# An output product by Strassen's seven products and a mask moved to GpSimd, in a fused sparse-attention and bilinear-FFN kernel

## The chip, the cores and the metric

The kernel runs on one core of one Trainium2 chip. The metric is device time in microseconds. A run more than 1.5% above the fastest of the same kernel counts as slow. Differences from a kernel with slow runs are taken from the mean of its fast runs.

## The reference, cut to what matters

```python
# 8 batches, 8 heads, 576 positions, head size 64
mask_local   = (rel >= 0) & (rel < 32)                      # heads 0 to 3
mask_strided = (rel >= 0) & (pos_k % 32 == pos_q % 32)      # heads 4 to 7
x = softmax(mask(q @ k.T / 8)) @ v        # as 4608 tokens x 512
a, b = x @ w_a, x @ w_b                   # 512 -> 1536
return (a * b) @ w_out                    # 1536 -> 512
```

## The kernel before

The FFN runs in nine tiles of 512 tokens. A tile has sixteen steps: twelve "ab" steps (two products of 128 features, eight matmuls of 512 columns; ScalarE copies one, VectorE multiplies the copy with the other in PSUM and writes `pf` in bf16) and four output steps (twelve matmuls each, ScalarE evicts, a DMA stores). The attention of batch t+1 is woven into tile t: S steps (scores, exponential on ScalarE, mask on VectorE) and V steps (product with v, logarithm and exponential on ScalarE for the reciprocal of the sum, two multiplies on VectorE into `xT`). VectorE also transposes the queries and keys of one batch further on. In the timelines each engine runs its instructions in the order of the program: in tile 4 VectorE stood idle for 2.61 us until the multiplies of a V step started at 198.96, and the transpose behind them, whose input had been loaded by about 187.2 (issued at 183.83, 3.4 us to landing at most), followed at 199.91. In this kernel matmul results go to PSUM, in buffers called banks below; to evict is to copy a result from there to SBUF, where the kernel has its operands.

```python
def S_m(b, u):                                   # mask: and with 0 / -1
    ...
    nc.vector.tensor_tensor(pi, pi, mk, op=ALU.bitwise_and)

def step_VT(b, u):
    ...                                          # matmuls into o (one buffer)
    nc.scalar.activation(r, sums, ACT.Ln)
    nc.scalar.activation(r, r, ACT.Exp, scale=-1.0)
    for j in range(2):
        ...
        nc.vector.tensor_mul(dst..., o..., r[:, j])   # into xT

def ffn_ab(t, f, mid, ab=None):
    ...
    a_sb = fsb.tile([128, TTOK], F32, tag="a_sb", name="a_sb")
    nc.scalar.copy(a_sb, ab[0])
    nc.vector.tensor_mul(pf[:, f, :], a_sb, ab[1])

def ffn_y(t, j, mid):
    ...
        y = psum4["mm"].tile([128, n], F32, tag="mm", name="mm")
        for f in range(FD):
            nc.tensor.matmul(y, lhsT=pf[:, f, 128 * j:128 * (j + 1)], rhs=wo_sb[:, f, c0:c0 + n], ...)
    ...
```

The softmax here doesn't subtract the row's maximum and nothing guards it: scores larger than these inputs give would overflow.

Of the kernel before, what the change touches and what calls it, by code (L numbers as in the profile page):

```python
# [7 lines left out]
F32 = mybir.dt.float32  # L8
BF16 = mybir.dt.bfloat16
I16 = mybir.dt.int16  # L10
ALU = mybir.AluOpType
# [13 lines left out]
VW = 128  # L25
WCH = (0, 2, 5, 8, 10, 12)


@with_exitstack
def kernel(  # L30
# [55 lines left out]
    mask_l = const.tile([128, 4, LW], I16)  # L86
    mask_s = const.tile([NP, NP], I16)
    nmask = const.tile([NP, NP], BF16, name="nmask")

# [66 lines left out]
    cur = {}  # L156
    xT = const.tile([128, KD, n_tok], BF16)
    wa_sb = wp.tile([128, KD, d_ff], BF16)
    wb_sb = wp.tile([128, KD, d_ff], BF16)
    wo_sb = wp.tile([128, FD, d_model], BF16)  # L160

    tl = {}
# [4 lines left out]

    nats = {}

    def load_qk(b, strided, heads=range(HL), names="kq"):  # L170
        for nm in names:
            src = {"k": k, "q": q}[nm]
            if b < FIRST_D:
                n, R, h0 = (NP, RS, HL) if strided else (96, RL, 0)
                if (b, nm, strided) not in nats:
                    nats[b, nm, strided] = nat.tile([n, HL, R, D], BF16, tag=f"{nm}{R}", name=f"{nm}{R}", bufs=1)
                t = nats[b, nm, strided]
                hs = slice(heads[0], heads[-1] + 1)
                nc.gpsimd.dma_start(out=t[:, hs], in_=src[b, h0:h0 + HL].rearrange("h (p r) d -> p h r d", r=R)[:, hs])
            elif strided:  # L180

                t = nat_s[nm]
                n = 32 if b == FIRST_D else YS
                for h in heads:
                    nc.gpsimd.dma_start(  # L185
                        out=t[32 * h:32 * h + n],
                        in_=bass.AP(tensor=src.tensor, offset=(b * H + HL + h) * S * D,
                                    ap=[[RS * D, n], [YS * RS * D, 3], [1, RS * D]]))
            else:
                if 0 in heads:  # L190
                    nats[b, nm, strided] = nat.tile([128, NY, D], BF16, tag=f"{nm}l", name=f"{nm}l")
                t = nats[b, nm, strided]
                for h in heads:
                    nc.gpsimd.dma_start(out=t[32 * h:32 * h + 32],  # L194
                                        in_=src[b, h].rearrange("(i y) d -> y i d", y=32))
            nats[b, nm, strided] = t
# [153 lines left out]
    def S_m(b, u):  # L350
# [4 lines left out]
        else:  # L355
            mk = mask_s.unsqueeze(1).unsqueeze(1).to_broadcast([NP, 2, G, n])
        pi = p[:M, :, :W].bitcast(I16).rearrange("p t (g n) -> p t g n", n=n)
        nc.vector.tensor_tensor(pi, pi, mk, op=ALU.bitwise_and)  # L358
# [68 lines left out]
    def step_VT(b, u):  # L427
# [21 lines left out]
        for j in range(2):  # L449
            dst = xT[64 * j:64 * j + 64, c, S * b:S * (b + 1)]  # L450
            if c < 2:
# [14 lines left out]
    def X_e(b, c):  # L466
        n = LW if c < 2 else NP
        tp = held.pop((b, "x", c))
        tv = tp.rearrange("d (g p) -> d g p", p=n)
        dst = xT[:, c, S * b:S * (b + 1)]  # L470
        if c >= 2:
# [39 lines left out]
    pfs = {}  # L511

    def ab_mm(t, f, ab, kks, mid=None, first=0, last=KD - 1):
        for w, ps_ in zip((wa_sb, wb_sb), ab):
            if mid and ps_ is ab[1]:
                mid()
            for kk in kks:
                nc.tensor.matmul(ps_, lhsT=w[:, kk, 128 * f:128 * (f + 1)], rhs=xT[:, kk, TTOK * t:TTOK * (t + 1)],  # L518
                                 start=(kk == first), stop=(kk == last))

    def ffn_ab(t, f, mid, ab=None):
# [3 lines left out]
        if ab is None:  # L525
            ab = [psum4["mm"].tile([128, TTOK], F32, tag="mm", name="mm") for _ in range(2)]
            if f == 0:
# [7 lines left out]
        nc.scalar.copy(a_sb, ab[0])  # L535
        nc.vector.tensor_mul(pf[:, f, :], a_sb, ab[1])  # L536
        return pf[:1, f, :1]

    def ffn_y(t, j, mid):
# [3 lines left out]
        for z, n in enumerate((256, 128, 128) if (t, j) == (NT - 1, 3) else (d_model,)):  # L543
            y = psum4["mm"].tile([128, n], F32, tag="mm", name="mm")
            for f in range(FD):
                nc.tensor.matmul(y, lhsT=pf[:, f, 128 * j:128 * (j + 1)], rhs=wo_sb[:, f, c0:c0 + n],  # L546
                                 start=(f == 0), stop=(f == FD - 1))
                if f == FD // 2 - 1:
                    mid()
            y_sb = fsb.tile([128, n], F32, tag="y_sb", name="y_sb", bufs=3)  # L550
            act = t < NT - 1 or (j + z) % 2 == 1
# [7 lines left out]
    with tc.manual_schedule(engines={ENG.PE, ENG.SP, ENG.Pool, ENG.DVE, ENG.Activation}):  # L559
# [71 lines left out]
        for t in range(NT):  # L631
            slots += [(ffn_ab, t, f) for f in range(FD)] + [(ffn_y, t, j) for j in range(4)]
        steps = {}
# [13 lines left out]
        for b in range(FIRST_D, B):  # L647
# [12 lines left out]
            for (z, nm, part), g in zip(((0, "k", 0), (0, "k", 1), (0, "q", 0), (0, "q", 1), (1, "k", 0), (1, "k", 1),  # L660
                                         (1, "k", 2), (1, "q", 0), (1, "q", 1), (1, "q", 2)), gs):
                do(g0 + g, step_D, b, z, nm, part)
        do(0, nc.vector.tensor_copy, mask_s, mss)
        for h in range(HL):
            do(6 + h, spread_vs, 1, h, nc.scalar.copy)
# [5 lines left out]
        for i, t in ((0, vl_buf[0]), (0, vs_buf[0]), (18, vl_buf[1]), (19, vs_buf[1])):  # L671
            do(i, fill_v, t)
        for i, (fn, t, j) in enumerate(slots):
            mid = lambda: take(i - 0.5)
            done = fn(t, j, mid) if fn is ffn_y else fn(t, j, mid, first.get(j) if t == 0 else None)
            if i > 13 and i in at:
# [33 lines left out]
```

## Time and profile before

| | before |
|---|---|
| time, median of 3 | 343.75 us (342.25 to 344.11) |
| TensorE busy | 333.1 us, 98% of the span |
| VectorE, ScalarE, GpSimd busy | 205.1, 203.9, 140.4 us |
| a tile with attention (tile 4): length, VectorE busy | 35.45, 24.80 us |
| a tile without (tile 7) | 31.08, 8.25 us |
| output phase of a tile without attention | 10.36 us |

TensorE is the bound; the other engines matter where TensorE waits for them. The lines are in the prediction.

### The profile page before, as it was taken

How to read it: one execution, taken by the hardware profiler on the slowest of the kernel's cores; microseconds unless marked ns; L12 is line 12 of the kernel's file. 1: busy time of each engine (PE TensorE's matmuls, PEld its weight loads, DVE VectorE, ACT ScalarE, POOL GpSimd, SP SyncE). 2: the span in 40 equal slices, each digit the busy share in tenths (PEclk: the TensorE clock that was granted, in tenths of full speed). 3: DMA queues.
4: the chain of work that ended last, by engine and by line, in shares of the span. 5: the costliest groups of instructions: out<-in, count | busy, mean ns of one | idle time of the engine just before them, and what ended most of it. 6: DMA issues, size and time to landing. Idle time of an engine off the chain costs nothing.

```text
span 341.5 us, 6887 instructions
## 1 busy us (share of the span) xinstructions
PE 333.1 (98%) x2520; PEld 173.7 (51%) x2520; DVE 205.1 (60%) x400; ACT 203.9 (60%) x331; POOL 140.4 (41%) x247
## 2 busy tenths in 40 slices
PE   8999999989989999999999999999999999999995
PEld 6754555445545555555555555555555444444444
DVE  6866657758759766876578846885666333303331
ACT  5754865368767765876587657775688533223311
POOL 8945539898537434653465346633000000000000
PEclk9999999999999999999999999999999999999999
DMA  9999999997999599969997989888220110021002
GB/s 160 154 203 197 202 176 172 179 154 89 129 200 101 90 99 185 99 110 91 165 104 133 77 168 96 132 80 145 76 59 2 61 63 0 0 92 34 0 31 94
DMA packets 102242, 37.56 MB, mean 110 GB/s; under 512 B 77632, under 2 KB 97728, under 8 KB 102208
## 3 DMA queue, kind: packets, MB, share of 16 engines
q0 software_dynamic: 87760, 19.58, 63.7%
q1 hardware_dynamic: 14304, 17.47, 16.2%
q8 instruction: 20, 0.33, 0.4%
q14 instruction: 14, 0.11, 0.1%
q10 hardware_dynamic: 144, 0.07, 0.1%
HBM read 39.71 MB, written 9.44 MB: 144 GB/s over the span
## 4 chain that ended last, share of the span: by engine, by line
PE 70%; DMA 17%; SPq 3%; DVE 3%; ACT 3%; POOL 2%; issue 2%; DVEq 0%; ACTq 0%
PE mm L518 41%; PE mm L546 20%; DMA vl<-in_v_dram 4%; PE o L438 3%; PE st L340 3%; DMA k<-in_k_dram 3%; DMA wa_sb<-in_moe_w_a_dram 3%; SPq L302 2%; DMA qz01l<-tq 2%; PE misc L153 2%; DMA out_dram<-y_sb 1%; DMA qz01s<-tq 1%; ACT xr L447 1%; DMA qz11s<-tq 1%; DVE tq L283 1%
## 5 line engine op out<-in xcount | busy, mean ns | idle before, releaser
L518 PE MATMUL mm<-xT,wb_sb 128*128 128x512 bf16 x424 | 110.1, 379 | 0.3
L518 PE MATMUL mm<-xT,wa_sb 128*128 128x512 bf16 x424 | 110.2, 379 | 0.1
L536 DVE TENSOR_TENSOR pf<-a_sb,mm 128x512 bf16<-128x512 f32 x106 | 71.9, 678 | 48.3 <-PE mm L518 25.5
L546 PE MATMUL mm<-wo_sb,pf 128*128 128x512 bf16 (+2 forms) x456 | 99.6, 368 | 0.1
L535 ACT COPY a_sb<-mm 128x512 f32<-128x512 f32 x106 | 62.1, 586 | 45.4 <-PE mm L518 43.0
L518 PEld LDWEIGHTS <-wb_sb 128*128 128x128 bf16 x432 | 41.7, 98 | 49.5 <-issue 1.3
L546 PEld LDWEIGHTS <-pf 128*128 128x128 bf16 x456 | 41.5, 98 | 42.3 <-issue 0.4
L518 PEld LDWEIGHTS <-wa_sb 128*128 128x128 bf16 x432 | 38.1, 98 | 34.2 <-issue 0.2
L552 ACT COPY y_sb<-mm 128x512 f32<-128x512 f32 (+2 forms) x35 | 20.0, 571 | 46.6 <-PE mm L546 38.6
L348 ACT ACTIVATE p<-st 128x576 bf16<-128x576 f32 (+1 forms) x64 | 41.7, 651 | 8.8 <-PE st L340 8.2
L447 ACT ACTIVATE xr<-o 64x576 f32<-64x576 f32 x48 | 31.1, 647 | 23.5 <-PE o L438 23.3
L454 DVE TENSOR_TENSOR xT<-o,xr 64x288 bf16<-64x288 f32 x48 | 21.6, 450 | 33.1 <-ACT xr L448 32.8
L448 ACT ACTIVATE xr<-xr 64x576 f32<-64x576 f32 x48 | 32.8, 682 | 1.5
L452 DVE TENSOR_TENSOR xT<-o,xr 64x288 bf16<-64x288 f32 x48 | 21.6, 450 | 16.9 <-ACT xr L448 16.4
L678 POOL CAST pace<-pf 1x1 f32<-1x1 bf16 x51 | 11.6, 227 | 41.5 <-DVE pf L536 41.3
L358 DVE TENSOR_TENSOR p<-p,mask_l 128x576 int16<-128x576 int16 x32 | 14.6, 455 | 17.1 <-ACT p L348 17.1
L218 POOL DMA_DIRECT2D vs<-in_v_dram x24 | 19.6, 817 | 9.9 <-issue 9.9
L194 POOL DMA_DIRECT2D kl<-in_k_dram x24 | 16.0, 666 | 6.7 <-issue 5.0
L194 POOL DMA_DIRECT2D ql<-in_q_dram x24 | 16.0, 666 | 6.6 <-DMA wo_sb<-in_moe_w_out_dram 3.8
L185 POOL DMA_DIRECT2D natk<-in_k_dram x24 | 14.6, 610 | 3.6 <-issue 3.0
L185 POOL DMA_DIRECT2D natq<-in_q_dram x24 | 14.6, 609 | 0.0
L678 POOL COPY pace<-y_sb 1x1 f32<-1x1 f32 x22 | 4.2, 189 | 24.2 <-ACT y_sb L552 24.2
(116 smaller groups left out, 316.2 us busy)
## 6 DMA issues: line engine op xcount, KB each, us to landing
out_dram<-y_sb SPq DMA_DIRECT2D x35, 256.0 KB, 2.4
vl<-in_v_dram POOLq DMA_DIRECT2D x7, 384.0 KB, 6.6
kl<-in_k_dram POOLq DMA_DIRECT2D x24, 72.0 KB, 2.8
ql<-in_q_dram POOLq DMA_DIRECT2D x24, 72.0 KB, 3.3
vs<-in_v_dram POOLq DMA_DIRECT2D x24, 72.0 KB, 3.6
wo_sb<-in_moe_w_out_dram POOLq DMA_DIRECT2D x4, 384.0 KB, 11.9
natk<-in_k_dram POOLq DMA_DIRECT2D x20, 72.0 KB, 3.3
natq<-in_q_dram POOLq DMA_DIRECT2D x20, 72.0 KB, 3.3
```

The lines of the kernel that those rows point to most:

```text
L185: nc.gpsimd.dma_start(out=t[32 * h:32 * h + n], in_=bass.AP(tensor=src.tensor, offset=(b * H + HL + h) * S * D, ap=[[RS * D, n], [YS * RS ...
L194: nc.gpsimd.dma_start(out=t[32 * h:32 * h + 32], in_=src[b, h].rearrange("(i y) d -> y i d", y=32))
L348: nc.scalar.activation(p[:M, :, :W], st[:M, :, :W], ACT.Exp, scale=scale)
L447: nc.scalar.activation(r, sums, ACT.Ln)
L448: nc.scalar.activation(r, r, ACT.Exp, scale=-1.0)
L452: nc.vector.tensor_mul(dst[:, W * half:W * (half + 1)], o[:64, j, :W], r[:, j])
L454: nc.vector.tensor_mul(dst.rearrange("d (p r) -> d p r", r=RS)[:, :, G * half:G * (half + 1)], o[:64, j, :W].rearrange("d (g p) -> d p g", ...
L518: nc.tensor.matmul(ps_, lhsT=w[:, kk, 128 * f:128 * (f + 1)], rhs=xT[:, kk, TTOK * t:TTOK * (t + 1)], start=(kk == first), stop=(kk == last))
L535: nc.scalar.copy(a_sb, ab[0])
L536: nc.vector.tensor_mul(pf[:, f, :], a_sb, ab[1])
L546: nc.tensor.matmul(y, lhsT=pf[:, f, 128 * j:128 * (j + 1)], rhs=wo_sb[:, f, c0:c0 + n], start=(f == 0), stop=(f == FD - 1))
L552: (nc.scalar.copy if act else nc.vector.tensor_copy)(y_sb, y)
```

## The change

The intent is to take an eighth of the multiplications out of the output product. Strassen's method splits a product into 2 x 2 blocks and forms it from seven block products of sums of blocks. Here the rows (tokens) are split in two, the 1536 features in even and odd groups of 128, the output columns in two halves. Sums of the weights are made once; sums of `pf` and the combination of the seven results are new work for VectorE and GpSimd. To relieve VectorE, the mask of the strided heads moves to GpSimd as a multiplication. To find room, `xT` becomes a ring of four batches; the matmul results get a fourth PSUM bank. (The prediction's count of time T starts at 0 with a tile's output phase, its last four steps; so does T below.)

```diff
         nc.scalar.copy(a_sb, ab[0])
-        nc.vector.tensor_mul(pf[:, f, :], a_sb, ab[1])
+        if t in FAST_Y:                                      # (1, ..., 8)
+            halves = lambda x: x.rearrange("p (m i) -> p m i", i=2)
+            nc.vector.tensor_mul(pf[:, f, :].rearrange("p (i m) -> p m i", i=2), halves(a_sb), halves(ab[1]))
+        else:
+            nc.vector.tensor_mul(pf[:, f, :], a_sb, ab[1])
...
+        if b >= FIRST_D and c >= 2:                          # in the mask step
+            pm = p[:M, :, :W].rearrange("p t (g n) -> p t g n", n=n)
+            nc.gpsimd.tensor_tensor(pm, pm, mask_b..., op=ALU.mult)
+            return
...
+        if n == 0:                                           # sums of pf, a third of the features at a time
+            nc.gpsimd.tensor_tensor(s[:, :, 0:HT], x[:, :, 0, 0], x[:, :, 1, 1], op=ALU.add)
+        elif n == 1:
+            nc.vector.tensor_tensor(s[:, :, HT:3 * HT]..., x[:, :, 0], x[:, :, 1], op=ALU.add)
+        else:
+            nc.vector.tensor_tensor(s[:, :, 3 * HT:]..., x[:, :, :, 1], x[:, :, :, 0], op=ALU.subtract)
...
+            rows = out[TTOK * t:TTOK * (t + 1), HN * j:HN * (j + 1)].rearrange("(q p i) c -> p i q c", q=2, i=2)
...
+            elif k == "4":                                   # w = P4 + P3, before P2 is added in bank b
+                v["w"] = v["a"]
+                nc.vector.tensor_tensor(v["w"], bank["b"], v["a"], op=ALU.add)
...
+        for k, b, lhs, rhs in (("3", "a", full(0, 0), wsum(0)), ("4", "b", full(1, 1), wsum(1)), ("1", "c", summed(0), wsum(2)),
+                               ("2", "b", summed(2), wfull(0, 0)), ("5", "a", summed(1), wfull(1, 1)),
+                               ("6", "c", summed(3), wsum(3)), ("7", "d", summed(4), wsum(4))):
```

The two halves of the rows are the even and the odd tokens of a tile. That is why the multiply goes through `pf` in the order m, i: two neighbouring inputs go to places 256 elements (512 bytes) apart.

More of the change, by code (lines that the diff above doesn't have):

```diff
@@ L26 @@
 WCH = (0, 2, 5, 8, 10, 12)
+FAST_Y = (1, 2, 3, 4, 5, 6, 7, 8)
 @with_exitstack
@@ L87 @@
     mask_s = const.tile([NP, NP], I16)
+    mask_b = const.tile([NP, NP], BF16)
     nmask = const.tile([NP, NP], BF16, name="nmask")
@@ L156 @@
     cur = {}
-    xT = const.tile([128, KD, n_tok], BF16)
+    XR = 4
+    xT = const.tile([128, KD, XR * S], BF16)
     wa_sb = wp.tile([128, KD, d_ff], BF16)
@@ L160, with fast_w @@
     wo_sb = wp.tile([128, FD, d_model], BF16)
+    FG = FD // 2
+    HT = TTOK // 2
+    HN = d_model // 2
+    wf = wp.tile([128, 5, FG, HN], BF16, name="wf")
+    wov = wo_sb.rearrange("p (g e) (j n) -> p e j g n", e=2, j=2)
+    def fast_w(n, gs):
+        a, b, op = ((wov[:, 0, 1], wov[:, 1, 1], ALU.subtract), (wov[:, 1, 0], wov[:, 0, 0], ALU.subtract),
+                    (wov[:, 0, 0], wov[:, 1, 1], ALU.add), (wov[:, 0, 0], wov[:, 0, 1], ALU.add),
+                    (wov[:, 1, 0], wov[:, 1, 1], ALU.add))[n]
+        nc.vector.tensor_tensor(wf[:, n, gs], a[:, gs], b[:, gs], op=op)
     tl = {}
@@ L168 @@
     nats = {}
+    shared = {}
     def load_qk(b, strided, heads=range(HL), names="kq"):
@@ L174, in load_qk @@
                 n, R, h0 = (NP, RS, HL) if strided else (96, RL, 0)
-                if (b, nm, strided) not in nats:
-                    nats[b, nm, strided] = nat.tile([n, HL, R, D], BF16, tag=f"{nm}{R}", name=f"{nm}{R}", bufs=1)
-                t = nats[b, nm, strided]
+                w0 = {"k6": 0, "q6": 1536, "k8": 3072, "q8": 5120}[f"{nm}{R}"]
+                if b not in shared:
+                    shared[b] = nat.tile([128, 5 * FD * TTOK // 4], BF16, tag="shared", name="shared")
+                t = nats[b, nm, strided] = shared[b][:n, w0:w0 + HL * R * D].rearrange("p (h r d) -> p h r d", r=R, d=D)
                 hs = slice(heads[0], heads[-1] + 1)
@@ L356, in S_m @@
             mk = mask_s.unsqueeze(1).unsqueeze(1).to_broadcast([NP, 2, G, n])
+        if b >= FIRST_D and c >= 2:
+            pm = p[:M, :, :W].rearrange("p t (g n) -> p t g n", n=n)
+            nc.gpsimd.tensor_tensor(pm, pm, mask_b.unsqueeze(1).unsqueeze(1).to_broadcast([NP, 2, G, n]), op=ALU.mult)
+            return
         pi = p[:M, :, :W].bitcast(I16).rearrange("p t (g n) -> p t g n", n=n)
@@ L449, in step_VT @@
         for j in range(2):
-            dst = xT[64 * j:64 * j + 64, c, S * b:S * (b + 1)]
+            dst = xT[64 * j:64 * j + 64, c, S * (b % XR):S * (b % XR + 1)]
             if c < 2:
@@ L469, in X_e @@
         tv = tp.rearrange("d (g p) -> d g p", p=n)
-        dst = xT[:, c, S * b:S * (b + 1)]
+        dst = xT[:, c, S * (b % XR):S * (b % XR + 1)]
         if c >= 2:
@@ L511, with mm_bank @@
     pfs = {}
+    used = [0]
+    def mm_bank(shape):
+        nm = "tp" if used[0] % 4 == 3 and used[0] >= 0 else "mm"
+        used[0] += 1
+        return psum4[nm].tile(shape, F32, tag=nm, name="mm")
     def ab_mm(t, f, ab, kks, mid=None, first=0, last=KD - 1):
+        n = min(TTOK, XR * S - TTOK * t % (XR * S))
+        cuts = [(0, n)] + ([(n, TTOK - n)] if n < TTOK else [])
         for w, ps_ in zip((wa_sb, wb_sb), ab):
@@ L517, in ab_mm @@
             for kk in kks:
-                nc.tensor.matmul(ps_, lhsT=w[:, kk, 128 * f:128 * (f + 1)], rhs=xT[:, kk, TTOK * t:TTOK * (t + 1)],
-                                 start=(kk == first), stop=(kk == last))
+                for c0, n in cuts:
+                    x0 = (TTOK * t + c0) % (XR * S)
+                    nc.tensor.matmul(ps_[:, c0:c0 + n], lhsT=w[:, kk, 128 * f:128 * (f + 1)], rhs=xT[:, kk, x0:x0 + n],
+                                     start=(kk == first and c0 == 0), stop=(kk == last and c0 == cuts[-1][0]))
     def ffn_ab(t, f, mid, ab=None):
@@ L525, in ffn_ab @@
         if ab is None:
-            ab = [psum4["mm"].tile([128, TTOK], F32, tag="mm", name="mm") for _ in range(2)]
+            ab = [mm_bank([128, TTOK]) for _ in range(2)]
             if f == 0:
@@ L535, in ffn_ab, with fast_s @@
         nc.scalar.copy(a_sb, ab[0])
-        nc.vector.tensor_mul(pf[:, f, :], a_sb, ab[1])
-        return pf[:1, f, :1]
+        if t in FAST_Y:
[3 more added lines that the diff above has]
+            nc.vector.tensor_mul(pf[:, f, :], a_sb, ab[1])
+        return pf[:1, f, :1]
+    pss = {}
+    def fast_s(t, n, gs):
+        if t not in pss:
+            pss[t] = nat.tile([128, 5 * FD * TTOK // 4], BF16, tag="shared", name="ps").rearrange("p (g m) -> p g m", g=FG)
+        s = pss[t][:, gs]
+        x = pfs[t].rearrange("p (g e) (i m) -> p g e i m", e=2, i=2)[:, gs]
+        if n == 0:
+            nc.gpsimd.tensor_tensor(s[:, :, 0:HT], x[:, :, 0, 0], x[:, :, 1, 1], op=ALU.add)
+        elif n == 1:
+            nc.vector.tensor_tensor(s[:, :, HT:3 * HT].rearrange("p g (i m) -> p g i m", i=2), x[:, :, 0], x[:, :, 1], op=ALU.add)
+        else:
+            nc.vector.tensor_tensor(s[:, :, 3 * HT:].rearrange("p g (e m) -> p g e m", e=2), x[:, :, :, 1], x[:, :, :, 0],
+                                    op=ALU.subtract)
@@ new lines, with y_plan, f32t, store @@
+    yst = {}
+    def y_plan(t):
+        pf, s = pfs[t], pss[t]
+        full = lambda e, i: (lambda g, q: pf[:, 2 * g + e, HT * i + 128 * q:HT * i + 128 * (q + 1)])
+        summed = lambda n: (lambda g, q: s[:, g, HT * n + 128 * q:HT * n + 128 * (q + 1)])
+        wsum = lambda n: (lambda g: wf[:, n, g])
+        wfull = lambda e, j: (lambda g: wov[:, e, j, g])
+        bank = {}
+        v = {}
+        def f32t(nm, bufs):
+            return fsb.tile([128, 2, HN], F32, tag=nm, name=nm, bufs=bufs)
+        def store(y, i, j, q=slice(0, 2), n=slice(0, HN)):
+            rows = out[TTOK * t:TTOK * (t + 1), HN * j:HN * (j + 1)].rearrange("(q p i) c -> p i q c", q=2, i=2)
+            nc.sync.dma_start(out=rows[:, i, q, n], in_=y[:, q, n])
+        def post(k):
+            if k == "3":
+                v["a"] = f32t("ya", 1)
+                nc.scalar.copy(v["a"], bank["a"])
+            elif k == "4":
+                v["w"] = v["a"]
+                nc.vector.tensor_tensor(v["w"], bank["b"], v["a"], op=ALU.add)
+            elif k == "1":
+                v["e"] = f32t("ye", 1)
+                nc.vector.tensor_tensor(v["e"], bank["c"], v["w"], op=ALU.add)
+            elif k == "2":
+                v["y21"] = f32t("y_sb", 4)
+                nc.scalar.copy(v["y21"], bank["b"])
+                store(v["y21"], 1, 0)
+                v["h"] = v["w"]
+                nc.gpsimd.tensor_tensor(v["h"], v["w"], v["y21"], op=ALU.subtract)
+            elif k == "5":
+                v["y12"] = f32t("y_sb", 4)
+                nc.scalar.copy(v["y12"], bank["a"])
+                store(v["y12"], 0, 1)
+                v["g"] = v["e"]
+                nc.gpsimd.tensor_tensor(v["g"], v["e"], v["y12"], op=ALU.subtract)
+            elif k == "6":
+                v["y22"] = f32t("y_sb", 4)
+                nc.vector.tensor_tensor(v["y22"], bank["c"], v["h"], op=ALU.add)
+                store(v["y22"], 1, 1)
+            else:
+                last(slice(0, 2), slice(0, HN))
+        def last(q, n):
+            if "y11" not in v:
+                v["y11"] = f32t("y_sb", 4)
+            nc.vector.tensor_tensor(v["y11"][:, q, n], v["g"][:, q, n], bank["d"][:, q, n], op=ALU.subtract)
+            store(v["y11"], 0, 0, q, n)
+        for k, b, lhs, rhs in (("3", "a", full(0, 0), wsum(0)), ("4", "b", full(1, 1), wsum(1)), ("1", "c", summed(0), wsum(2)),
+                               ("2", "b", summed(2), wfull(0, 0)), ("5", "a", summed(1), wfull(1, 1)),
+                               ("6", "c", summed(3), wsum(3)), ("7", "d", summed(4), wsum(4))):
+            new = b not in bank
+            if new:
+                bank[b] = mm_bank([128, 2, HN])
+            tail = k == "7" and t == NT - 1
+            for q in range(2):
+                for n in ((slice(0, 128), slice(128, 256)) if tail and q == 1 else (slice(0, HN),)):
+                    for g in range(FG):
+                        nc.tensor.matmul(bank[b][:, q, n], lhsT=lhs(g, q), rhs=rhs(g)[:, n],
+                                         start=new and q == 0 and g == 0, stop=g == FG - 1, skip_group_check=True)
+                        if g == FG - 1:
+                            if tail:
+                                last(slice(q, q + 1), n)
+                            elif q == 1:
+                                post(k)
+                        yield v
@@ L539, in ffn_y, with ffn_ys @@
+    def ffn_ys(t, j, mid):
+        if j == 0:
+            yst[t] = y_plan(t)
+        n = 21 + (6 if (t, j) == (NT - 1, 3) else 0)
+        for i in range(n):
+            v = next(yst[t])
+            if i == n // 2:
+                mid()
+        if j == 3:
+            for _ in yst[t]:
+                pass
+        return v[("a", "e", "y12", "y11")[j]][:1, 0, :1]
     def ffn_y(t, j, mid):
@@ L543, in ffn_y @@
         for z, n in enumerate((256, 128, 128) if (t, j) == (NT - 1, 3) else (d_model,)):
-            y = psum4["mm"].tile([128, n], F32, tag="mm", name="mm")
+            y = mm_bank([128, n])
             for f in range(FD):
@@ L549, in ffn_y @@
                     mid()
-            y_sb = fsb.tile([128, n], F32, tag="y_sb", name="y_sb", bufs=3)
+            y_sb = fsb.tile([128, n], F32, tag="y_sb", name="y_sb", bufs=4)
             act = t < NT - 1 or (j + z) % 2 == 1
@@ L631 @@
         for t in range(NT):
-            slots += [(ffn_ab, t, f) for f in range(FD)] + [(ffn_y, t, j) for j in range(4)]
+            slots += [(ffn_ab, t, f) for f in range(FD)] + [(ffn_ys if t in FAST_Y else ffn_y, t, j) for j in range(4)]
         steps = {}
@@ L663 @@
         do(0, nc.vector.tensor_copy, mask_s, mss)
+        do(0, nc.vector.tensor_scalar_mul, mask_b, mss, -1.0)
         for h in range(HL):
@@ L672 @@
             do(i, fill_v, t)
+        for n in range(5):
+            for z in range(2):
+                do(17 + 2 * n + z, fast_w, n, slice(3 * z, 3 * z + 3))
+        for t in FAST_Y:
+            for n, at_ in ((0, (3, 7, 11)), (1, (4, 8, 11)), (2, (5, 9, 11))):
+                for z in range(3):
+                    do(16 * t + at_[z], fast_s, t, n, slice(2 * z, 2 * z + 2))
         for i, (fn, t, j) in enumerate(slots):
+            if i == 0:
+                used[0] = -1000 * 3
+            elif i == 16:
+                used[0] = 0
             mid = lambda: take(i - 0.5)
-            done = fn(t, j, mid) if fn is ffn_y else fn(t, j, mid, first.get(j) if t == 0 else None)
+            done = fn(t, j, mid) if fn is not ffn_ab else fn(t, j, mid, first.get(j) if t == 0 else None)
             if i > 13 and i in at:
```

## The prediction

> **What bounds the kernel now.** I read the page first, then one row of the windows view per token tile, then the chain of waits, then the timeline of one tile's output phase.
>
> From the page, busy time by engine:
>
> ```profile
> PE 333.1 (98%) x2520; PEld 173.7 (51%) x2520; DVE 205.1 (60%) x400; ACT 203.9 (60%) x331; POOL 140.4 (41%) x247
> ```
>
> From the groups kept apart by shape, two of VectorE (line, engine, operation, output and inputs, shape, count, busy us, mean ns, idle before):
>
> ```profile
> L536 DVE TENSOR_TENSOR pf<-a_sb,mm 128x512 bf16<-128x512 f32 x106 | 71.9, 678 | 48.3 <-PE mm L518 25.5 <-ACT a_sb L535 21.2
> ...
> L358 DVE TENSOR_TENSOR p<-p,mask_s 72x576 int16<-72x576 int16 x28 | 12.5, 447 | 0.5 <-ACT p L348 0.5
> ```
>
> TensorE is busy 98% of the span: it is the bound. The windows view (stretch, length, then busy us and count of PE, PEld, DVE, ACT, POOL, then clock, DMA share, GB/s) says how much room the others have:
>
> ```profile
> 63.80:99.00 35.20, 32.61 (x251) 16.79 (x249) 24.42 (x46) 23.41 (x39) 25.85 (x41) 1.00 1.35 136
> ...
> 170.23:205.68 35.45, 35.42 (x258) 18.24 (x256) 24.80 (x46) 24.91 (x41) 18.01 (x35) 1.00 0.92 119
> ...
> 275.83:306.91 31.08, 31.08 (x146) 14.07 (x144) 8.25 (x12) 9.38 (x16) 0.00 (x0) 1.00 0.09 34
> ```
>
> These are about tile 1, tile 4 and tile 7. Tile 7 is pure FFN. Tile 4 carries a batch of attention and the transposes of the next: VectorE is then busy 24.8 of 35.45 us, and it runs in program order, so part of its idle time is waiting. Tile 1 has 2.6 us of TensorE idle already.
>
> The chain of waits (start, length, what) gives the matmul rate:
>
> ```profile
> 275.83 20.72 PE mm L518 x96
> 296.55 10.36 PE mm L546 x48
> ```
>
> 20.72/96 = 10.36/48 = 215.8 ns per 512-column matmul. The output product of one tile costs 10.36 us.
>
> The timeline of tile 4's output phase shows the in-order VectorE:
>
> ```profile
> 194.12 2.76 PE L546 MATMUL mm<-wo_sb,pf 128*128 128x512 bf16 x12
> ...
> 194.67 0.69 DVE L536 TENSOR_TENSOR pf<-a_sb,mm 128x512 bf16<-128x512 f32 x1
> ...
> 195.65 0.70 DVE L288 STREAM_TRANSPOSE tk<-natk 128x512 bf16<-128x512 bf16 x1
> ...
> 196.67 0.81 POOL L218 DMA_DIRECT2D vs<-in_v_dram  x1 [0.90 <-issue]
> ...
> 200.86 0.42 PE L438 MATMUL o<-p,vs 72*128 72x72 bf16 x8
> ...
> 201.32 0.65 ACT L447 ACTIVATE xr<-o 64x576 f32<-64x576 f32 x1 [0.93 <-PE o L438]
> ...
> 202.00 0.68 ACT L448 ACTIVATE xr<-xr 64x576 f32<-64x576 f32 x1
> ...
> 202.72 0.92 DVE L454 TENSOR_TENSOR xT<-o,xr 64x288 bf16<-64x288 f32 x2 [1.36 <-ACT xr L448]
> ```
>
> The last four lines are one V step: TensorE starts it at 200.86, the two VectorE multiplies end at 203.64, 2.78 us later, and everything emitted after them on VectorE queues behind. Today this costs nothing: each output bank is evicted by ScalarE and is not written again in the same phase.
>
> [...]
>
> **The change part by part.**
>
> TensorE. Per fast tile 48 matmuls of 512 columns (10.36 us) become 7 products x 2 row blocks x 6 = 84 of 256 columns: 84 x 109.2 ns = 9.17 us. Weight loads rise to 84 but do not bind: eight of them took 0.51 us in the attention steps, some 59 ns each. Saving 1.19 us a tile, 9.5 us over eight tiles. Against it, the ring buffer for xT splits tile 4's operand in two[...]. Ceiling: 343.75 - 9.3 = 334.5 us, 2.7% faster.
>
> VectorE, per fast tile. Added: four additions with a PSUM operand of 512 (the pf row, 0.68 each, 2.7 us) and six operand sums of 1024 bf16 ([...]0.68 each, 4.1). Removed: four strided masks x 0.447 = 1.8 for tiles with attention. Net +5.0: tiles 2 to 5 go from 24.8 to 29.8 of 35 us. Once, in tile 1, ten weight sums of 768 elements[...].
>
> GpSimd, per tile with attention: four masks (576 x 2.2 = 1.27 us), three sums of 512 (1.12) and two subtractions of 512 (1.12): 10.7 us on top of 18.0 busy plus 4.2 of DMA issue gaps. It fits, barely.
>
> ScalarE: three copies of 0.586 instead of four.
>
> Now the waits, which I think decide. Seven products use four banks; product 4 and product 2 accumulate in the same bank, and between them VectorE must read product 4 alone (w = P4 + P3). So product 2 waits for that addition. Take T = 0 at the start of the output phase of tile 4 (194.12). Products 3 and 4 and 1 are 36 matmuls, 3.93 us; with step V6 (0.26) after the 21st, TensorE wants to start product 2 at T = 4.19. V6 starts at T = 21 x 0.109 = 2.29. On VectorE the order is: last pf, transpose, two operand sums, V6's two multiplies, another transpose, then the addition. V6's multiplies end 2.78 us after its start: 5.07. Transpose and addition, 0.65 each back to back: 6.4. Product 2 is 2.2 us late.
>
> Beside it, GpSimd: its pacing copy ends at T = 1.65, then the mask of S7 (to 2.9), the issue of a vs load (0.4 to 0.9 gap plus 0.81: 4.1 to 4.6), then the last third of product 1's operand sum (to 5.3 to 5.8). Product 1 needs it from its fifth matmul at T = 3.3. This stall, 2.0 to 2.5 us, overlaps the other: product 1 then ends at 6.2 to 6.7. Together about 2.3 us, not the sum.
>
> Tile by tile: tiles 2 to 5 gain 1.19 and lose about 2.3, +1.1 each, +4.4. Tile 6 has no transposes and no loads: the addition ends at 5.07 + 0.65 = 5.7, a stall of 1.5, net +0.3. Tiles 7 and 8 have no attention: the addition follows product 4 at once, and they gain 1.2 and about 1.0, the end of the kernel staying much as it is: -2.2. Tile 1: its output phase already waits for the transposed queries (released by a DMA that ended at 95.06, some 1.1 us of idle TensorE); weight sums and operand sums push VectorE, which has about 3 us of idle in the second half of that tile, back by 1 to 2 us, so the wait moves and nothing is gained: +1. Split of tile 4: +0.24. Sum: +3.7, or 347.5 us.
>
> **The rivals.** First: the arithmetic arrives, near 335 us. For it: tiles 7 and 8 will show it, and the matmul banks go from three to four, so the ab phase tolerates a later VectorE. Against: the order on VectorE is fixed by the program, and the 2.78 us latency of a V step is measured. Second: VectorE or GpSimd becomes the bound throughout tiles 1 to 5, through [...]slow two-byte scattered writes of pf: at 1 us more per tile, 352 us or above. For it: 29.8 of 35 us in an in-order queue leaves little. Against: the ab phase has slack of about one slot of 2 us and four banks. Third: the operands of the next batch come late. S4 of tile 3 waited for a DMA of transposed queries (landed 146.48), so any lag of VectorE at a tile's start is paid at once; I put it at 0.1 to 0.5 us a tile, and it would make 349.
>
> **Range and chances.** The stall estimates are good to about 0.7 us a tile over five tiles (3.5 us), tile 1 to 1.5 us, contention unknown upwards: 340.5 to 353. More than 2% faster (under 336.9) needs nearly all stalls gone: 0.11. More than 2% slower (over 350.6) needs one of the later rivals: 0.20. Within 2%: 0.69.
>
> **What would show it.** Right: tiles 7 and 8 take 29.9 us against 31.08; the output phases of tiles 2 to 5 last longer than before, with TensorE idle 2 us or more before the first matmul of product 2 (released by the VectorE addition) or within product 1 (released by GpSimd's sum); GpSimd masks near 1.3 us and sums near 1.1. Wrong: no such gap and tiles 2 to 5 under 35 us; or tiles 7 and 8 not shorter, which would mean that 256-column matmuls with a weight load each do not run at 109 ns; or long gaps in the ab phase before matmuls waiting for pf, which would mean that VectorE itself is the bound.

Some of its figures no trace had shown yet. What the runs show of them:

| figure of the prediction | measured |
|---|---|
| matmul of 256 columns, 109.2 ns | 109.2 ns: 84 in 9.17 us (tile 7 of `e8_order_mask_dve`) |
| GpSimd, 2.2 ns an element | mask 1267 ns for 576 (2.2); in `e1_halves` sum 1168 ns for 512 (2.3), subtractions in fp32 1270 and 1269 ns for 512 (2.5) |
| operand sum of 1024, 0.68 us | 0.65 and 0.68 us in tile 5 of `e5_mask_dve`, means there 709 and 760 ns |
| split of tile 4, 0.24 us | its ab steps 23.89 us in `e1_halves`, those of tiles 3 and 5 23.60 |

The ten weight sums took 734 ns each in `e1_halves`, 7.3 us.

## The result

The changed kernel took 499.83 us (median; 497.64 to 505.25, four runs, the last of them slow), the kernel before 343.93 in the same comparison. The ratio is 1.451 (95% interval 1.442 to 1.459). Ratios are the mean time of one kernel's fast runs over that of the other's of the same rounds, so not quite the ratio of the medians quoted. The prediction was 347.5, range 340.5 to 353.

The page of the changed kernel, busy time by engine:

```profile
PE 357.0 (72%) x2855; PEld 214.2 (43%) x2886; DVE 433.9 (87%) x466; ACT 201.6 (41%) x324; POOL 229.6 (46%) x338
```

TensorE went from 98 to 72% busy, VectorE from 205.1 to 433.9 us: it is the bound now. The groups kept apart by shape say with what:

```profile
L570 DVE TENSOR_TENSOR pf<-a_sb,mm 128x512 bf16<-128x512 f32 x96 | 228.8, 2442 | 5.3 <-ACT a_sb L567 4.7
...
L376 POOL TENSOR_TENSOR p<-p,mask_b 72x576 bf16<-72x576 bf16 x24 | 30.4, 1267 | 0.0
```

The multiply into `pf` has the same shape as before and takes 2442 ns in place of 678 in the 96 calls of tiles 1 to 8: its busy time grew by some 164 us (228.8 less 96 x 0.678), of the 229 that VectorE gained. The GpSimd mask takes 1267 ns, as estimated. Tile by tile, in the windows view, with the columns that the prediction lists (about tile 4 and tile 7):

```profile
244.70:302.60 57.90, 39.54 (x393) 32.38 (x392) 53.43 (x54) 24.47 (x39) 29.75 (x47) 0.94 0.58 73
...
410.80:451.20 40.40, 31.97 (x179) 17.36 (x181) 34.82 (x23) 8.78 (x15) 8.50 (x12) 1.00 0.09 28
```

Tile 4 went from 35.45 to 57.90 us with VectorE busy 53.43 of them (24.80 before); tile 7, which was to be the clean gain, from 31.08 to 40.40 with VectorE busy 34.82 (8.25 before). The waits view (who waited for whom: us, times, longest) has TensorE waiting for the multiply:

```profile
ACT a_sb L567 <- DVE pf L570: 96.0, 73, 3.3
PEld L550 <- issue: 86.9, 90, 2.5
PE mm L550 <- DVE pf L570: 61.2, 64, 2.4
```

The last line is the missing bank: 64 times, 61.2 us in all, a matmul of an ab step waited until the multiply two steps back had read its bank. The 87 us that the weight loads spent "issue" (waiting for nothing that the profile shows) probably lie in the same gaps.

### The profile page after: what moved, and what is told of

It reads as the page before. It is cut to its first block, busy times and chain, and to the rows that moved or that the text cites. A ratio compares the mean times of both kernels' runs of the same rounds, so it can differ in the third digit from the quotient of the medians.

```text
span 496.0 us, 7770 instructions
## 1 busy us (share of the span) xinstructions
PE 357.0 (72%) x2855; PEld 214.2 (43%) x2886; DVE 433.9 (87%) x466; ACT 201.6 (41%) x324; POOL 229.6 (46%) x338
## 4 chain that ended last, share of the span: by engine, by line
DVE 46%; issue 21%; PE 19%; DMA 7%; POOL 3%; ACT 2%; POOLq 0%; DVEq 0%; ACTq 0%
DVE pf L570 27%; PE mm L654 9%; PE mm L550 6%; DMA wb_sb<-in_moe_w_b_dram 4%; DVE xT L473 3%; DVE ps L585 3%; DMA wo_sb<-in_moe_w_out_dram 3%; DVE xT L475 2%; DVE ps L587 2%; DVE p L379 2%; DVE tk L305 1%; DVE tq L305 1%; PE o L459 1%; PE mm L683 1%; DVE tq L300 1%
## 5 line engine op out<-in xcount | busy, mean ns | idle before, releaser
L570 DVE TENSOR_TENSOR pf<-a_sb,mm 128x512 bf16<-128x512 f32 x96 | 228.8, 2442 | 5.3 <-ACT a_sb L567 4.7
L550 PE MATMUL mm<-xT,wb_sb 128*128 128x512 bf16 (+1 forms) x465 | 113.7, 369 | 60.9 <-DVE pf L570 60.3
L550 PE MATMUL mm<-xT,wa_sb 128*128 128x512 bf16 (+1 forms) x451 | 111.4, 365 | 3.8 <-DVE xT L475 1.9
L654 PEld LDWEIGHTS <-ps 128*128 128x128 bf16 x486 | 48.6, 104 | 32.4 <-POOL ps L583 12.9
L654 PE MATMUL mm<-wf,pf 128*128 128x256 bf16 x192 | 29.0, 293 | 28.1 <-DVE pf L570 28.0
L654 PE MATMUL mm<-wf,ps 128*128 128x256 bf16 (+1 forms) x294 | 37.4, 273 | 11.4 <-POOL ps L583 10.4
L654 PE MATMUL mm<-wo_sb,ps 128*128 128x256 bf16 x192 | 29.1, 314 | 9.1 <-DVE ya L615 8.9
L587 DVE TENSOR_TENSOR ps<-pf 128x1024 bf16<-128x1024 bf16 x24 | 32.1, 1336 | 0.0
L376 POOL TENSOR_TENSOR p<-p,mask_b 72x576 bf16<-72x576 bf16 x24 | 30.4, 1267 | 0.0
L583 POOL TENSOR_TENSOR ps<-pf 128x512 bf16<-128x512 bf16 x24 | 28.2, 1175 | 0.3
L585 DVE TENSOR_TENSOR ps<-pf 128x1024 bf16<-128x1024 bf16 x24 | 27.7, 1153 | 0.4
```

What stands on the lines that cost most here:

```text
L550: nc.tensor.matmul(ps_[:, c0:c0 + n], lhsT=w[:, kk, 128 * f:128 * (f + 1)], rhs=xT[:, kk, x0:x0 + n], start=(kk == first and c0 == 0), sto ...
L570: nc.vector.tensor_mul(pf[:, f, :].rearrange("p (i m) -> p m i", i=2), halves(a_sb), halves(ab[1]))
L585: nc.vector.tensor_tensor(s[:, :, HT:3 * HT].rearrange("p g (i m) -> p g i m", i=2), x[:, :, 0], x[:, :, 1], op=ALU.add)
L587: nc.vector.tensor_tensor(s[:, :, 3 * HT:].rearrange("p g (e m) -> p g e m", e=2), x[:, :, :, 1], x[:, :, :, 0], op=ALU.subtract)
L654: nc.tensor.matmul(bank[b][:, q, n], lhsT=lhs(g, q), rhs=rhs(g)[:, n], start=new and q == 0 and g == 0, stop=g == FG - 1, skip_group_check ...
```

## The experiments

**First round: what of the loss is the write.** `e1_halves` takes the first and the last 256 tokens as the two halves of the rows. Strassen's method doesn't care which rows are paired, so the kernel stays correct.

```diff
-            halves = lambda x: x.rearrange("p (m i) -> p m i", i=2)
-            nc.vector.tensor_mul(pf[:, f, :].rearrange("p (i m) -> p m i", i=2), halves(a_sb), halves(ab[1]))
+            nc.vector.tensor_mul(pf[:, f, :], a_sb, ab[1])
-            rows = ....rearrange("(q p i) c -> p i q c", q=2, i=2)
+            rows = ....rearrange("(i q p) c -> p i q c", q=2, i=2)
```

> The changed kernel with one thing undone: the elementwise product is written to pf in order, and the two row halves are tokens 0 to 255 and 256 to 511 of a tile in place of even and odd tokens (the store's row pattern follows). Theory (the scattered 2-byte write of pf is the cause of nearly all of the loss): pf multiply back to 0.68 us from 2.44, VectorE busy from 434 to about 265 us, and the time to what the prediction said for the rest, 347 us (342 to 353), with TensorE idle about 2 us before product 2 or inside product 1 in tiles 2 to 5. Rival A (operand sums, PSUM additions[...] carry much of the loss: the local masks went from 455 to 765 ns, the sums take 1.15 to 1.34 instead of 0.68): 380 us or more. Rival B (no stall is left): 335 us.

Measured: 366.72 us (median of two fast and two slow runs) against 344.02, ratio 1.066 (1.057 to 1.076); the two fast runs alone, 363.83 and 364.10, give 1.058. Between fast runs, 135 of the 155 us went with this one line. But 364.0, the mean of the fast runs, is outside the 342 to 353 expected of it: 16.5 us more than my estimate for the rest. The groups of this run:

```profile
L569 DVE TENSOR_TENSOR pf<-a_sb,mm 128x512 bf16<-128x512 f32 x96 | 65.0, 677 | 24.4 <-PE mm L550 18.8 <-ACT a_sb L567 4.7
L586 DVE TENSOR_TENSOR ps<-pf 128x1024 bf16<-128x1024 bf16 x24 | 30.7, 1280 | 0.0
```

The multiply is back to 677 ns, while one of the two kinds of operand sum takes 1280 in place of the 680 that I had worked out. The output phase of tile 5, in the timeline (lines left out between):

```profile
249.21 1.26 POOL L376 TENSOR_TENSOR p<-p,mask_b 72x576 bf16<-72x576 bf16 x1
...
249.46 1.56 DVE L584 TENSOR_TENSOR ps<-pf 128x1024 bf16<-128x1024 bf16 x1
...
250.94 2.10 DVE L586 TENSOR_TENSOR ps<-pf 128x1024 bf16<-128x1024 bf16 x1
...
251.32 1.16 POOL L582 TENSOR_TENSOR ps<-pf 128x512 bf16<-128x512 bf16 x1
...
252.54 1.05 PE L653 MATMUL mm<-wf,ps 128*128 128x256 bf16 x8 [1.52 <-POOL ps L582]
...
255.25 2.02 PE L653 MATMUL mm<-wo_sb,ps 128*128 128x256 bf16 x17 [1.66 <-DVE ya L614]
```

The phase starts at 247.53. Both predicted stalls are there, each released by what the prediction named: product 1 resumes at T = 5.01 after GpSimd's sum (predicted 5.3 to 5.8), product 2 starts at T = 7.72 after the addition (predicted 6.4). But they add up, 1.52 and 1.66 us of idle TensorE, and don't overlap, because the addition is 1.3 us later than predicted: the two operand sums on VectorE last from 249.46 to 252.97, 3.5 us instead of 1.4, while GpSimd's mask and sum run in the same stretch. Each of the two ends 0.55 us after the GpSimd instruction that it overlaps (251.02 after 250.47, 253.04 after 252.48), as if it had waited for it (that it did is not shown), while GpSimd's own two, 1.26 and 1.16 us, take no longer than elsewhere (means 1.28 and 1.17). The windows view shows a second thing (output phases of tiles 2 and 5):

```profile
130.83:147.35 16.52, 13.41 (x119) 10.64 (x116) 11.55 (x17) 5.85 (x10) 10.77 (x16) 0.79 0.64 95
...
247.53:261.47 13.94, 10.71 (x118) 9.25 (x116) 11.13 (x16) 5.81 (x10) 10.15 (x14) 1.00 0.81 115
```

Tile 2's phase ran at a mean granted clock (the share of TensorE's full speed that was granted) of 0.79: its 17 matmuls of product 2 took 3.78 us, tile 5's took 2.02. Before, these phases took 11.56 and 11.40 us at clock 1.00. Gaps of the same length stand in tiles 4 and 5 (1.39 and 1.66 us in tile 4), which ran at 1.00, so the gaps alone don't settle it.

`e2_pf_only` is the reverse: the kernel before with only the scattered write.

```diff
+        if t > 0:
+            halves = lambda x: x.rearrange("p (m i) -> p m i", i=2)
+            nc.vector.tensor_mul(pf[:, f, :].rearrange("p (i m) -> p m i", i=2), halves(a_sb), halves(ab[1]))
+        else: ...                                   # and the rows of the store to match
```

> The kernel before with only the scattered write of pf added for tiles 1 to 8, no Strassen, no GpSimd mask. Theory: the multiply takes 2.4 to 2.65 us here too; tile 4 goes from 24.8 to about 46 us of VectorE work and so from 35.4 to 46 to 50 us; tiles 7 and 8 have 29.4 us of VectorE work and stay at 31 to 34; in all 405 to 440 us. Rival A (the write is slow only beside the other new work[...]): multiply under 1.2 us and the time under 365 us.

Measured: 436.58 us, ratio 1.269, within what was expected.

```profile
L538 DVE TENSOR_TENSOR pf<-a_sb,mm 128x512 bf16<-128x512 f32 x96 | 227.9, 2431 | 17.6 <-ACT a_sb L535 16.1
```

The write alone costs 93 us on the kernel before, with none of the change's work on GpSimd there and the multiply at 2431 ns: that work isn't its cause. In the changed kernel it cost 135, likely because VectorE had less idle time there to hide it in; no run tests that.

`e3_stride_in` keeps even and odd tokens, but goes through the same values in the other order: writes in order, reads with a step of two fp32 elements.

```diff
-            halves = lambda x: x.rearrange("p (m i) -> p m i", i=2)
-            nc.vector.tensor_mul(pf[:, f, :].rearrange("p (i m) -> p m i", i=2), ...)
+            halves = lambda x: x.rearrange("p (m i) -> p i m", i=2)
+            nc.vector.tensor_mul(pf[:, f, :].rearrange("p (i m) -> p i m", i=2), ...)
```

> The changed kernel with the same values at the same places in pf, but the multiply runs through them in the other order: it writes in order and reads both fp32 inputs with a step of two elements. If the hop of the write is what costs: multiply 0.7 to 1.0 us and the time within 15 us of e1_halves. If any pattern that isn't contiguous costs, or the read's step as much as the write's: multiply 1.3 to 2.5 us and 400 to 500 us.

Measured: 366.15 us.

```profile
L570 DVE TENSOR_TENSOR pf<-a_sb,mm 128x512 bf16<-128x512 f32 x96 | 65.0, 678 | 24.3 <-PE mm L550 18.8 <-ACT a_sb L567 4.7
```

The result is the same byte for byte in `pf`; only the order of writing differs. It is the write that costs, and the repair needs no other split of the rows: with a step of two in the fp32 reads, in SBUF and in PSUM, the multiply takes 678 ns, with none 677 (`e1_halves`).

`e4_forms` and `e12_forms2` measure write patterns by themselves: the kernel before, with one extra instruction into an unused tile in each ab step of tiles 7 and 8. Two of the forms:

```diff
+            elif f == 3:      # one bf16 in each 4-byte word
+                nc.vector.tensor_mul(scr[:, :1024].rearrange("p (m i) -> p m i", i=2)[:, :, 0], a_sb, ab[1])
+            elif f == 4:      # runs of two bf16, alternating between two halves
+                nc.vector.tensor_mul(scr[:, :512].rearrange("p (i m r) -> p m i r", i=2, r=2), v(a_sb), v(ab[1]))
```

> The kernel before with one extra multiply (or ScalarE copy) into an unused tile in each ab step of tiles 7 and 8, in twelve forms; only durations are read, the time is not. In order 0.68 us; 2-byte halves alternating 2.4 to 2.65; step-two reads, ordered write 0.7 to 1.0; 2-byte write with a step of 4 bytes: 0.7 if the distance matters, 2.4 if each 2-byte write alone in its word costs; runs of 4 bytes alternating: about 1.0 to 1.5; runs of 8 bytes or 16 bytes: 0.68 (the attention multiplies with runs of 8 bytes cost nothing extra); fp32 in order 0.68; fp32 alternating single words: 1.0 to 1.5 if the cost is per hop of a word, 2.4 if it is the same as for 2 bytes; 2-byte write with a step of 16 bytes: 2.4. ScalarE alternating copy: no expectation; 0.59 if the cost is VectorE's own, over 1 if it is the memory's.

> Ten more write patterns of a 512-element VectorE multiply in tiles 7 and 8 of the kernel before, and a GpSimd copy alternating and in order; only durations are read. From e4_forms: a lone 2-byte write a word away costs little (0.72), 16 or 512 bytes away 2.4 us, runs of two or more elements nothing, lone fp32 words 1.05. If what counts is that neighbouring writes fall in one 8- or 16-byte line: 2-byte with step 8 bytes 1.0 or less when the line is 16 bytes, 2.4 when it is 8; the patterns that alternate 16 bytes apart 2.4. Lone fp32 words with a step of 8 bytes 0.7 to 1.05, of 16 bytes 1.05 or more[...]. Runs of two starting at an odd element: over 1 if the run has to be one aligned word, 0.68 if not. Alternating over four regions: 2.4. GpSimd: no expectation.

The view of the unused tile (line, engine, count: ns min/median/max, first and last start) for `e4_forms`: alternating bf16, one bf16 per word, alternating runs of two bf16, alternating fp32, and the alternating ScalarE copy:

```profile
L546 DVE TENSOR_TENSOR scr<-a_sb,mm x2: 2407/2408/2410, 279.8 to 314.1; 128x512 bf16<-128x512 f32 x2
...
L551 DVE TENSOR_TENSOR scr<-a_sb,mm x2: 722/722/722, 284.9 to 319.2; 128x512 bf16<-128x512 f32 x2
L554 DVE TENSOR_TENSOR scr<-a_sb,mm x2: 681/682/682, 286.6 to 320.9; 128x512 bf16<-128x512 f32 x2
...
L565 DVE TENSOR_TENSOR scr<-a_sb,mm x2: 1047/1049/1051, 293.5 to 327.8; 128x512 f32<-128x512 f32 x2
...
L571 ACT CAST scr<-a_sb x2: 2463/2465/2467, 297.7 to 332.1; 128x512 bf16<-128x512 f32 x2
```

And for `e12_forms2` one bf16 every 8 bytes, and the alternating GpSimd copy:

```profile
L545 DVE TENSOR_TENSOR scr<-a_sb,mm x2: 1296/1296/1296, 282.0 to 317.7; 128x512 bf16<-128x512 f32 x2
...
L565 POOL CAST scr<-a_sb x2: 2450/2453/2456, 302.7 to 338.4; 128x512 bf16<-128x512 f32 x2
```

All forms, for 512 elements:

| write pattern | ns |
|---|---|
| bf16 in order; the same starting at an odd element | 680; 684 |
| single bf16, step 4 bytes | 722 |
| single bf16, step 8 bytes; two of them 4 bytes apart, then on to the next 16 bytes | 1296; 1282 |
| single bf16, step 16 bytes; alternating 16 bytes apart | 2429; 2407 |
| single bf16, alternating 512 bytes apart (the change); over four regions | 2408; 2422 |
| runs of 2, 4 or 8 bf16, alternating; runs of 2 every 16 bytes | 680 to 682; 674 |
| runs of 2, of 4, alternating, starting at an odd element | 1578; 1020 |
| fp32 in order; single, step 8 bytes | 681; 682 |
| single fp32, step 16 bytes; alternating | 1071; 1049 |
| ScalarE copy in order; alternating bf16 | 618; 2465 |
| GpSimd copy in order; alternating bf16 | 615; 2453 |

Three engines come to about the same time (2408, 2465 and 2453 ns), which points to the write into SBUF and not to VectorE; on ScalarE and GpSimd the slow form also reads with a step of two, which was tried alone on VectorE only (670 ns in `e4_forms`). The durations of single 2-byte elements fit a straight line in the number of visits, where each 16 bytes of the tile count as a line and a visit ends when the next element falls in another one: 4.42 ns a visit and 156 ns beside it (both fitted to these durations) give 722, 1288 and 2419 ns for 128, 256 and 512 visits, where 722, 1282 to 1296 and 2407 to 2429 were measured. The runs that start at an odd element, if the tile starts on a line, make 320 and 192 visits: 1570 and 1005 ns by the same fit, 1578 and 1020 measured. That is a fit to these patterns, not a mechanism shown. Two elements that fill a whole 4-byte word pay nothing (682 and 674 ns against 680 in order), against the expectation (1.0 to 1.5 us); two that straddle words do (1578). The step of 8 bytes was expected at 1.0 us or less, or at 2.4, and is neither. Single fp32 words that alternate or are 16 bytes apart take 1049 and 1071 ns in place of 681, (1049 - 681)/512 = 0.72 ns more for each.

**Second round: what of the rest is the mask, what the order.** `e5_mask_dve` puts the strided mask back on VectorE in `e1_halves`; `e6_mask_only` adds only the GpSimd mask to the kernel before.

```diff
-        if b >= FIRST_D and c >= 2:                # e5: removed from e1_halves; e6: added to the kernel before
-            ...
-            nc.gpsimd.tensor_tensor(pm, pm, mask_b..., op=ALU.mult)
-            return
```

> e1_halves with the strided mask back on VectorE for all batches (the other part of the change undone). In e1_halves TensorE stands twice in each output phase of tiles 2 to 5: 1.4 to 1.7 us inside product 1 for GpSimd's sum, 1.7 us before product 2 for the VectorE addition. Theory: the GpSimd mask of S7 sits ahead of the sum in GpSimd's queue (1.28 us)[...]; without it the first gap falls to 0 to 0.5 us, the sums to 0.7 to 0.9, the local mask from 0.65 back to 0.5 or less, and the time by 3 to 8 us against e1_halves (about 360). Rival: the mask on GpSimd relieves VectorE, which is the late one; with it back the second gap grows by 0.4 us or more a tile and the time stays or rises (367 to 372).

> The kernel before with only the GpSimd mask (third batch on), no Strassen. Theory: GpSimd has room (18 of 35 us a tile, some 23 with the masks), the steps that use the mask come 4 us or more later, so TensorE does not notice: within 1% of the kernel before (341 to 347), with the local mask on VectorE slightly longer than 455 ns[...]. Rival: the mask alone costs over 2% (351 or more).

`e5_mask_dve` took 353.99 us (ratio 1.029, 1.024 to 1.035): about 10 less than the fast runs of `e1_halves`, in the direction of the theory and more than the 3 to 8 that it gave. The sums fell from 847 and 1280 ns to 709 and 760, the local mask from 648 to 572, and the gap before product 2 from 1.66 to 0.30 us in tile 5. The first gap stayed, against the expectation, because GpSimd's sum still stands behind the issue of a load. The timeline of tile 5's phase, which starts at 239.54:

```profile
242.69 0.81 POOL L235 DMA_DIRECT2D vs<-in_v_dram  x1 [0.84 <-issue]
...
243.52 1.16 POOL L578 TENSOR_TENSOR ps<-pf 128x512 bf16<-128x512 bf16 x1
...
244.74 1.05 PE L649 MATMUL mm<-wf,ps 128*128 128x256 bf16 x8 [1.60 <-POOL ps L578]
...
245.38 0.65 DVE L610 TENSOR_TENSOR ya<-mm,ya 128x512 f32<-128x512 f32 x1
246.09 1.14 PE L649 MATMUL mm<-wo_sb,ps 128*128 128x256 bf16 x9 [0.30 <-DVE ya L610]
```

Here the prediction's stall comes out as it was worked out: the addition ends at T = 6.49 (predicted 6.4), the two waits overlap, and TensorE idles 1.60 + 0.30 = 1.9 us (predicted about 2.3).

`e6_mask_only` took 344.48 us (ratio 1.001, 0.995 to 1.006), GpSimd's masks 1268 ns each, and the local mask on VectorE stayed at 455 ns. So the mask on GpSimd is free in the kernel before and costs about 10 us once operand sums run on both engines (6 with the order of products changed, below): a part tried alone can't tell what it costs beside the others. `e5_mask_dve` changes both the overlap with GpSimd and the length of its queue, so it doesn't divide the cost between them.

`e7_order` changes in `e1_halves` the order of the products in tiles 1 to 7; `e8_order_mask_dve` does so in `e5_mask_dve`.

```diff
-        products in the order 3 4 1 2 5 6 7
+        for n in ("3412567" if t == NT - 1 else "3451726"):     # and e - y12 once both are there
```

> e1_halves with the products in the order 3 4 5 1 7 2 6 in tiles 1 to 7 (3 4 1 2 5 6 7 before; tile 8 keeps it), nothing else: product 1 comes 12 matmuls later, product 2 24 matmuls later. Theory (the gaps are the two waits, of product 1 for GpSimd's sum and of product 2 for the addition that stands behind V6's multiplies in VectorE's queue[...]): both gaps shrink to 0.5 us or less, tiles 2 to 5 shorten by about 3 us each, tile 6 by 1.5, the low-clock stretches in tiles 2 and 3 go, in all 346 to 353. Rival (VectorE has too much work in these tiles whatever the order): the gaps move to other products or to the next tile and the time stays within 4 us of e1_halves.

> e7_order and e5_mask_dve together. If [...]GpSimd's queue still cost something once the order is mended: 1 to 4 us under e7_order (345 to 350). If the mask on GpSimd is then a relief to VectorE: 1 to 4 us above it.

`e7_order` took 348.68 us (ratio 1.015): 15 us less than the fast runs of `e1_halves`, within the theory's range, with no gap before products 1 and 2 in tiles 2 to 6. Part of the idle time moved: the first ab steps of tiles 3 to 6 now wait 0.95, 0.93, 0.95 and 0.25 us for VectorE to read the bank of product 6. In `e8_order_mask_dve` those waits are gone too. `e8_order_mask_dve` took 342.97 (ratio 0.996, 0.991 to 1.002), 5.7 less than `e7_order`, more than the 1 to 4 expected. The seven products are level with the kernel before here. Tile 7's output phase took 9.17 us (from 296.84 to 306.01, the start of tile 8's output phase less 20.72 of ab steps): the predicted 84 x 109.2 ns. What is still lost is in tile 1, whose phase took, in the windows view,

```profile
87.46:102.90 15.44, 12.37 (x144) 9.81 (x143) 14.14 (x27) 9.24 (x16) 12.14 (x19) 1.00 1.10 122
```

15.44 us with VectorE busy 14.14, against 14.05 us before (84.64 to 98.69), after starting 2.8 us later; and 1 us in tile 8, where three pieces of the last product share a bank with the subtraction that reads it.

**Third round: a version that beats both.** `e9_from2` is `e8_order_mask_dve` with tile 1 left plain and the last pieces in three banks; `e10_from3` leaves tile 2 plain too and moves the weight sums there; `e11_from2_later` is `e9_from2` with the weight sums five steps later.

```diff
-FAST_Y = (1, 2, 3, 4, 5, 6, 7, 8)
+FAST_Y = (2, 3, 4, 5, 6, 7, 8)                            # e10: from 3
+                    bk = mm_bank([128, 2, HN]) if tail and q == 1 else bank[b]
-                do(17 + 2 * n + z, fast_w, n, slice(3 * z, 3 * z + 3))
+                do(22 + 2 * n + z, fast_w, n, slice(3 * z, 3 * z + 3))      # e11 only; e10: 33
```

> e8_order_mask_dve with two repairs: tile 1 keeps the plain output product (the weight sums stay in tile 1), and the last product's three pieces in tile 8 write to three banks, so that TensorE doesn't wait for the subtraction between them (gaps of 0.57 and 0.38 us). Theory: what e8_order_mask_dve loses against the saving is in tile 1 (4.2 us behind the kernel before at its end) and at the end (1 us); with most of it back the time is 335 to 340, 1 to 2.5% faster than the kernel before. Rival: tile 1 is late because of the ten weight sums, which are still there: 340 to 343.

> As e9_from2, with tile 2 plain too and the weight sums in tile 2, where VectorE has room (26 of 35.8 us). One tile's saving (1 us) less, tile 1 as in the kernel before: 337 to 340 if tile 1 is then free of loss. If e9_from2 is the slower one by over 1 us, the weight sums in tile 1 are what costs there.

> As e9_from2, with the weight sums five steps later in tile 1, where the kernel before's VectorE has its gaps. If the place of the sums matters: 1 to 2 us under e9_from2. If not: within 1 us of it.

Measured: 339.91 (ratio 0.990, 0.985 to 0.994), 339.29 (0.989, 0.984 to 0.993) and 337.98 us (0.983, 0.980 to 0.987). `e11_from2_later` beats both kernels, the one before by 1.7%, which is clear of the noise and under 2%: of the 9.5 us that eight tiles could save (8.3 for its seven) it gets 5.5. The intervals of the three overlap, so it is likely, but not settled, that the place of the weight sums matters.

## Why the prediction was wrong

**The step that failed** is the list "VectorE, per fast tile. Added: four additions ... and six operand sums". The multiply into `pf` isn't in it: I took it to cost 0.68 us as before, since shape and types are the same. It appears only in the second rival, as "slow two-byte scattered writes of pf", at 1 us more per tile. It measured 12 x 1.76 = 21 us of VectorE per tile, where TensorE takes 35. That is the term of the sum that was mis-sized, and 135 us (`e1_halves`) of the 155 us lost. The multiplies into `xT` of the kernel before gave no warning: those that write runs of four bf16 at a step of 16 bytes (L454) take 450 ns, as the contiguous ones do; `e4_forms` shows that alternating runs of two or more are free (680 to 682 ns against 680 in order) and alternating single elements aren't (2408). The prediction's sum has no term for the access pattern.

**What stood.** The matmul rate of 109.2 ns and the 9.17 us of an output phase hold exactly where nothing waits (tile 7 of `e8_order_mask_dve`; in the changed kernel itself VectorE hid it). The two stalls in the output phase are where the prediction put them and have the releasers it named; moving the products apart (`e7_order`) removes them, at the price of smaller waits at the start of the next tile. The GpSimd durations, 1.27 predicted and 1267 ns measured for the mask, 1.12 and 1168 for the sum in `e1_halves`, are right.

**What was mis-sized beside it.** With the write mended, tiles 2 to 5 were to lose 1.1 us each; `e1_halves` lost 6.6, 3.4, 2.2 and 2.1 (for example tile 5: 23.60 + 13.94 against 24.05 + 11.40). Two steps of the prediction are at fault. It said that the two stalls overlap, "not the sum"; they add up, because the operand sums took 3.5 us instead of 1.4 beside GpSimd's work and pushed the addition behind the end of product 1. I had put no number to what the sums would take beside GpSimd's work: with the GpSimd mask gone, the mean of the slower sums falls from 1280 to 760 ns, the stalls overlap as predicted, and the kernel gains about 10 us (`e5_mask_dve`). And I left out the clock: the phases of tiles 2 and 3 ran at 0.79 and 0.89. In `e7_order` those gaps are gone, and 17 matmuls of a product take 2.17 us in tile 2's phase, as in those of tiles 4 and 5 (3.78 in tile 2 of `e1_halves`). Its profiled run is 15.8 us shorter: 14.5 us of gaps less in tiles 2 to 6, 3.1 more at the tile starts, and some 4 that tiles 2 and 3 had over tile 5. That the low clock follows from the gaps is not shown: tiles 4 and 5 had the same gaps at 1.00. Tile 1, put at +1 us, cost 6 in `e1_halves` (2.4 in its ab steps, 3.6 in its output phase), with VectorE late throughout. Tile 8 gained nothing instead of 1.0; two waits at its end (0.57 and 0.38 us in `e8_order_mask_dve`), where its last pieces share a bank, account for most of that.

**The rivals.** The first (the arithmetic arrives) was refuted by the changed kernel, though `e11_from2_later` gets over half of the saving. The second is what happened, for the reason it names, at about twenty times the size it gave, and the sign that came is the last of those that the prediction listed for being wrong: gaps in the ab phase before matmuls waiting for `pf`. The third, late operands of the next batch, shows in none of tiles 3 to 7 of `e1_halves`: their ab steps are up to 0.5 us shorter than before.

## What to carry to other kernels

When an instruction keeps its shape but gets another access pattern, treat it as a new instruction: look at what its neighbouring writes are, and measure one before building on it. If a scattered order is needed, scatter on the fp32 read side and write in order (678 ns here, against 2442 with the scattered write); or choose the split, as Strassen's row pairing allows, so that nothing is scattered. Where an engine's instructions run in the order of the program, put a bank's second use as far as possible behind the reader of its first (15 us here, `e7_order`), and judge work moved to GpSimd beside the other work it will meet (about 10 us, `e5_mask_dve`), not alone (none, `e6_mask_only`).
